# Copying shared rows two pairs ahead, and making the zeros for the first products first

## The chip, the core and the metric

The kernel runs on one core of a Trainium2 chip. The core has a matrix engine (TensorE, in the profile PE, with its weight loads as PEld), a vector engine (VectorE, DVE), a scalar engine (ScalarE, ACT), a general engine (GpSimd, POOL) and an engine that here only starts transfers (SyncE, SP). Each works through its own queue of instructions in order, and they wait for one another through semaphores. Data comes from the main memory (HBM) into SBUF by DMA; matrix products land in PSUM. The metric is the device time in microseconds (us) of one execution; the median of several executions is compared.

## What is computed

Attention over 64 pairs of batch and head, with a window of 32 keys (half of the heads) or every fourth of 128 keys (the other half), and then a mixture of experts with one expert per token. The expert is either the one that the token's own gate prefers or the one of the token before it.

```python
scores = scale * np.matmul(q, k.transpose(0, 1, 3, 2))
mask_plain = (rel >= 0) & (rel < window)
mask_dil = (rel >= 0) & (rel < window * dilation) & (rel % dilation == 0)
...
attn = np.exp(scores)
attn = attn / (np.sum(attn, axis=-1, keepdims=True) + 1e-09)
x = np.matmul(attn, v)
...
for b in range(B):
    prev_e = -1
    for s in range(S):
        fresh_e = int(np.argmax(logits[b, s]))
        if s == 0 or local_gate[b, s] < 0.5:
            e = fresh_e
        else:
            e = prev_e if prev_e >= 0 else fresh_e
        prev_e = e
        h = np.maximum(x[b, s] @ w1[e], 0.0)
        out[b, s] = p[e] * (h @ w2[e])
```

Batch 8, 8 heads of 64, 576 positions, so 4608 tokens of 512 features; 8 experts with 1024 hidden features; everything in 32-bit floats.

## The kernel before, in words

The heads are taken in pairs: there are 32 pairs of heads (`NPB`), each with its 576 positions in 9 blocks of 64. The heads with the wide window are reordered on the host, so that every head needs only a narrow band: a block of 64 queries looks at 96 keys, its own 64 and the 32 before them.

The function `whole` runs the kernel once with `exact` false; its result says whether a second, slower pass is needed, which a branch then runs (it isn't taken with this data). All of PE, DVE, POOL and SP are scheduled by hand: in each queue the instructions stand in the order in which the Python code makes them. The array `ones` is made ahead of that region, on DVE (L203). At the start of `whole`, DVE makes `zero` (L251), which POOL writes into one spare row of two buffers in the main memory (L253), and POOL clears a strip of the four `vt` tiles (L257). DVE then makes `warm`, an array of zeros of 128 by 512 (L281), and PE multiplies it by itself three times (`WARM`, L283) into a bank that nobody reads, before the first keys have come. After that DVE makes `before` (L300).

The attention loop (L1091) has one turn for each pair, and two more. In turn n, `scores(n)` multiplies keys and queries of pair n (L322 adds masks, L329), DVE and ACT make the exponentials `pr` (L334, L336); `share(n)` copies on POOL; then come `values(n - 1)`, the products of the exponentials with `vt` (L381), which DVE divides by their sums (L385, L386) into `x`. In every second turn `turn` transposes `x` on PE (L402, L406; ACT copies the result, L403), and `store` writes it to the main memory. `load(n + 3)` starts the transfers of keys and values three pairs ahead, from SP. The tile `vt` holds, for each block, 96 rows of values: the 64 rows of the block come by DMA, and the 32 rows ahead of it are the last ones of the block before. They are copied within SBUF by `share` (L270), one copy of 32 by 1040 elements for each pair. Four `vt` tiles are used in turn (`AHEAD`).

Between these steps `gap` takes steps of the routing from a list (`waiting`), by hand-written costs: gate logits (L433), the choice of experts (L445 to L516), the gates (L524 to L530), places within the expert (L540 and L541 on PE into the bank `kp`, L543 to L583 on DVE), and at two points the table of tokens for each expert. After the second of four groups of batches, the tokens of the first two units of expert work are known (`tokens`, L710 to L730), and the list `rows` is filled with eight gathers: POOL starts indirect DMAs that fetch rows of `x` by token number from the main memory into `xg` (L847). One gather is taken from the list at the end of each turn (L1116). So in the last turns of the attention loop POOL's queue has, in alternation, one copy (`share`) and one gather. PE uses the first four gathers in the last turn (L862), the others after the first expert's hidden products (L917).

The expert phase multiplies by the weights of the experts, 256 tokens at a time, with sums that save one product in eight (L943, L1025 with L810 to L819 on DVE).

The four PSUM banks of the attention phase are handed out in turn to `pv`, `tp`, `kp` and the other results of the routing; a product has to wait until the reader of the bank's earlier content is done.

Of the kernel before, what the change touches and what calls it, by code (L numbers as in the profile page):

```python
# [10 lines left out]
F32 = mybir.dt.float32  # L11
# [11 lines left out]
P = 128  # L23
# [14 lines left out]
NPB = B * NP  # L38
# [143 lines left out]
@with_exitstack  # L182
def dilated_attn_locality_moe_kernel(
    ctx: ExitStack,
    tc: tile.TileContext,
    qk: bass.AP,
    v: bass.AP,
    wgl: bass.AP,
    w1: bass.AP,
    w2: bass.AP,  # L190
    con: bass.AP,
    adm: bass.AP,
    msk: bass.AP,
    qmk: bass.AP,
    out: bass.AP,
):
    nc = tc.nc
    keep = ctx.enter_context(tc.tile_pool(name="keep", bufs=1))
    cst = keep.tile([P, C_ALL], F32, name="cst")
    wg = keep.tile([P, DK, LW], F32, name="wg")  # L200
    ones = keep.tile([P, P], F32, name="ones")
    bad = keep.tile([1, 1], I32, name="bad")
    nc.vector.memset(ones, 1.0)  # L203

    args = (qk, v, wgl, w1, w2, con, adm, msk, qmk, out, cst, wg, ones)
    again = whole(tc, False, bad, *args)

    with tc.If(again > 0):  # L208
        whole(tc, True, bad, *args)


@with_exitstack
def whole(ctx, tc, exact, bad, qk, v, wgl, w1, w2, con, adm, msk, qmk, out, cst, wg, ones):
    nc = tc.nc
    name = "exact" if exact else "plain"
    ctx.enter_context(tc.manual_schedule(engines={ET.PE, ET.DVE, ET.Pool, ET.SP}))
# [14 lines left out]
    def room(to, i, name, shape):  # L231
# [9 lines left out]
    ins, work, xp, xtp = (attention.enter_context(tc.tile_pool(name=name, bufs=bufs))  # L241
                     for name, bufs in (("ins", AHEAD), ("work", 2), ("xp", 3), ("xtp", 2)))
# [3 lines left out]
    def bank(shape, name):  # L246
        return banks.tile(shape, F32, name=name, tag="bank")
# [20 lines left out]
    def share(n):  # L268
        vt = vts[n % AHEAD]
        nc.gpsimd.tensor_copy(vt[:WIN, :, 1:], vt[QB:, :, :NB - 1])  # L270

    def load(n):
        load_keys(n)
        load_values(n)

    if not exact:
        am = work.tile([P, adm.shape[1]], BF16, name="am", bufs=1)
        nc.sync.dma_start(out=am, in_=adm)
        mk = work.tile([KW, 2, S - UNITS[1][0] * QB], BF16, name="mk", bufs=1)
        warm = work.tile([P, 512], F32, name="warm", bufs=1)  # L280
        nc.vector.memset(warm, 0.0)  # L281
        for _ in range(WARM):
            nc.tensor.matmul(bank([P, 512], "cold"), lhsT=warm[:, :P], rhs=warm, start=True, stop=True)  # L283
    load_keys(0)
# [17 lines left out]
    def load_first(i, part):  # L302

        rows = FK // 4
        nc.sync.dma_start(out=raw1[i][:, part * rows:(part + 1) * rows].rearrange("p m k f -> p (m k f)"),
                          in_=w1[i, :, part * rows * D:(part + 1) * rows * D])
# [60 lines left out]
    def values(n):  # L367

        vt = loaded[n][2]
        if n % 2 == 0:  # L370
            xs[n // 2] = xp.tile([P, SLOTS, 2, 2, DH], F32, name="x")
        x = xs[n // 2]
        pr = prob.pop(n)
        for a, z in HALVES:
            pv = bank([P, z - a, 2, VW], "pv")
            for k in range(a, z):
                for u in range(2):
                    for h in range(2):
                        i = min(2 * k + h, NB - 1)
                        c, p = next((c, p) for c, p in reversed(pr) if c <= i)  # L380
                        nc.tensor.matmul(pv[h * QB:(h + 1) * QB, k - a, u], lhsT=p[:, u, (i - c) * QB:(i - c + 1) * QB],  # L381
                                         rhs=vt[:, u, i], start=True, stop=True, tile_position=(0, h * QB),
                                         skip_group_check=True)
            r = rec[:, n, a:z]
            nc.vector.reciprocal(r, pv[:, :, :, DH])  # L385
            nc.vector.tensor_tensor(x[:, a:z, n % 2], pv[:, :, :, :DH],  # L386
                                    r.unsqueeze(3).to_broadcast([P, z - a, 2, DH]), op=Alu.mult)
        del loaded[n]

    def turn(m):  # L390

        x = xs[m]
        b, g = divmod(m, 2)
        if m % (2 * GB) == 0:
            routes[b // GB] = dict(xt=xtp.tile([P, 2, CH, GS], F32, name="xt"))
        xt = routes[b // GB]["xt"]
        s = b % GB * S
        full = S // P * P
        for c in range(CH):
            tp = bank([P, S // P, P], "tp")  # L400
            for k in range(S // P):
                nc.tensor.transpose(tp[:, k], x[:, k, c].rearrange("p u d -> p (u d)"), ident)  # L402
            nc.scalar.copy(xt[:, g, c, s:s + full], tp.rearrange("p k t -> p (k t)"))  # L403
        tp = bank([P, CH, S - full], "tp")
        for c in range(CH):
            nc.tensor.transpose(tp[:, c], x[:S - full, S // P, c].rearrange("p u d -> p (u d)"),  # L406
                                ident[:S - full, :S - full])
        nc.scalar.copy(xt[:, g, :, s + full:s + S], tp)

    def store(m):  # L410

        x = xs.pop(m)
        b, g = divmod(m, 2)
        full = S // P * P
        to = xd[g][b * S:(b + 1) * S]
        nc.sync.dma_start(out=to[:full].rearrange("(k p) f -> p k f", p=P),
                          in_=x[:, :S // P].rearrange("p k g u d -> p k (g u d)"))
        nc.sync.dma_start(out=to[full:], in_=x[:S - full, S // P].rearrange("p g u d -> p (g u d)"))
# [360 lines left out]
    def gap(add=None):  # L779
        if add is not None:  # L780
            credit[0] = min(credit[0] + add, add)
        alone = False
        while waiting and not alone and (add is None or credit[0] >= 0):
            f, cost, _ = waiting.pop(0)
            credit[0] -= cost
            if f:
                f()
            alone = add is None or not waiting or waiting[0][2]
# [7 lines left out]
    def now(push):  # L796
        for f in push:
            f()
# [55 lines left out]
    def features(u):  # L854
        kind = units[u]["kind"]
        rows = rows_in(u)
        xe[u] = mw.tile([P, DK, 2 * P], F32, name="xe")
        for j in range(tiles_of(u)):
            x = xg.pop((u, j)).rearrange("p g f -> p (g f)")
            tp = bank([P, DK, P], "tp")  # L860
            for kk in range(DK):
                nc.tensor.transpose(tp[:, kk, :rows], x[:rows, kk * P:(kk + 1) * P], ident[:rows, :rows])  # L862
            nc.scalar.copy(xe[u][:, :, j * P:j * P + rows], tp[:, :, :rows])
        if kind == "pair":
            xc[u] = mw.tile([P, 4, DK // 2, P], F32, name="xc", bufs=1)
            return sums_right(xc[u], *(xe[u][:, 2 * k:2 * k + 2, j * P:(j + 1) * P]
                                       for k in range(2) for j in range(2)))
        return []
# [222 lines left out]
    for n in range(NPB + 2):  # L1091
        if n < NPB:
            (scores_exact if exact else scores)(n)
        if n < NPB:
            share(n)
        gap(SHARE)
        if 1 <= n <= NPB:
            values(n - 1)
        if n == NPB + 1:
            assert len(rows) <= 4  # L1100
            now(features(0))
        if n >= 3 and n % 2 == 1:
            turn((n - 3) // 2)
            if (n - 3) // 2 % (2 * GB) == 2 * GB - 1:
                route((n - 3) // 2 // (2 * GB), n == NPB + 1)
        gap(SHARE)
        if n + 3 < NPB:
            load(n + 3)
        if n >= 3 and n % 2 == 1:
            store((n - 3) // 2)  # L1110
        if n in (11, 14, 17, 20):
            load_first(0, (n - 11) // 3)
        if n == NPB + 1:
            weights(0, True)
            weights(1, False)
        if rows:  # L1116
            rows.pop(0)()
# [161 lines left out]
```

## Time and profile before

| | |
|---|---|
| median of 3 executions | 675.02 us (674.6 to 676.7) |
| the profiled execution | 672.8 us |
| its span, first to last instruction | 670.9 us |
| mean granted PE clock in it | 0.995 of full |
| bytes by DMA, mean rate | 126.38 MB, 188 GB/s |

The attention phase takes the span's first 158 us or so, the experts the rest. A line of the timeline gives the start (us from the span's start), the length, the engine, the line of the kernel, the operation, its output and inputs, how many of them were merged, and in brackets how long the engine had been idle before and what ended that. In a list of waits, each line names who waited for whom, then us in total, how many times, and the longest. In a table of windows each line is a stretch of time with the busy time of each engine in it, the granted clock of PE (1.00 is full), the share of time in which the DMA engines were busy, and what they moved.

The start of the kernel on DVE, in the timeline (the three arrays, then `before`):

```profile
0.85 0.17 DVE L203 MEMSET ones<- 128x128 f32 x1 [0.85 <-PEq L1271]
1.01 0.27 DVE L251 MEMSET zero<- 1x256 f32 x1
1.33 0.48 DVE L281 MEMSET warm<- 128x512 f32 x1
1.77 0.07 DVE L300 MEMSET before<- 96x8 f32 x1
```

And on PE, the first products and the first scores:

```profile
1.87 4.78 PE L283 MATMUL cold<-warm 128*128 128x512 f32 x6 [1.87 <-DVE before L300]
6.58 0.34 PE L322 MATMUL two<-am 64*96 64x320 bf16 x2
6.76 1.67 PE L329 MATMUL two<-kq 64*96 64x64 f32 x36
```

### The profile page before, as it was taken

To read this page: it belongs to the slowest core of one execution; us is meant where nothing else is said; L and a number is where in the kernel's file an instruction comes from. 1 tells how busy PE (TensorE), PEld (TensorE's weight loads), DVE (VectorE), ACT (ScalarE), POOL (GpSimd) and SP (SyncE) were. 2 spreads that over 40 slices of the span, in tenths; PEclk is the share of its full clock that TensorE was granted. 3 is DMA by queue.
4 is the path that set the end of the run, shared out by engine and by line. 5 is a ranking of instruction groups with operands and counts; after the bars stand their busy time and mean duration, and the time that the engine had idled before them with its cause. 6 is when DMAs were issued, how large, how long until landed. Compare 5 with 4: busy or idle time off the path is not lost. (4 is left out here: it accounts for less than half of the span.)

```text
span 670.9 us, 15284 instructions
## 1 busy us (share of the span) xinstructions
PE 655.1 (98%) x6466; PEld 572.1 (85%) x6466; DVE 373.7 (56%) x755; ACT 188.7 (28%) x348; POOL 186.6 (28%) x162
## 2 busy tenths in 40 slices
PE   8999999999999999999999999999999999999996
PEld 6988888787769999999589989997889988899893
DVE  3548669474397587363455581727373637446441
ACT  3544343432112232322223213222222232213210
POOL 3322212132023420321560343414044213041011
PEclk9999999999999999999999999999999999999999
DMA  8989889746403289666452545741054452353001
GB/s 325 321 274 310 279 263 324 244 138 240 196 33 146 91 355 386 228 221 214 140 233 75 219 173 185 288 143 60 9 189 166 182 218 98 123 221 145 1 33 49
DMA packets 29357, 126.38 MB, mean 188 GB/s; under 512 B 4221, under 2 KB 13789, under 8 KB 25312
## 3 DMA queue, kind: packets, MB, share of 16 engines
q1 hardware_dynamic: 22480, 106.10, 43.7%
q0 software_dynamic: 6800, 19.21, 8.3%
q8 instruction: 53, 0.87, 0.5%
q14 instruction: 24, 0.20, 0.1%
HBM read 142.07 MB, written 19.20 MB: 240 GB/s over the span
## 5 line engine op out<-in xcount | busy, mean ns | idle before, releaser
L971 POOL DMA_INDIRECT out_dram<-y,tok x36 | 55.0, 1528 | 297.0 <-DVE y L1040 124.0
L943 PE MATMUL hp<-xc,sum 128*128 128x128 f32 x720 | 85.6, 276 | 0.4 <-DVE sum L810 0.4
L943 PEld LDWEIGHTS hp<-xc,sum 128*128 128x128 f32 x720 | 82.8, 192 | 0.8 <-PE hp L943 0.5
L1025 PE MATMUL yp<-sum,hc 128*128 128x256 f32 x360 | 82.7, 380 | 0.0
L953 DVE TENSOR_TENSOR h<-hp,h 128x512 f32<-128x512 f32 x45 | 30.9, 690 | 90.4 <-PE hp L943 89.7
L1025 PEld LDWEIGHTS yp<-sum,hc 128*128 128x128 f32 x360 | 68.3, 190 | 9.6 <-ACT y L1033 0.4
L1040 DVE SCALAR_TENSOR_TENSOR y<-yp,gate,y 128x256 f32<-128x256 f32 x45 | 21.7, 482 | 75.3 <-issue 48.1
L270 POOL COPY vt<-vt 32x1040 f32<-32x1040 f32 x32 | 34.5, 1081 | 95.8 <-DMA vt<-in_v_dram 67.8
L943 PE MATMUL hp<-xe,raw 128*128 128x128 f32 x480 | 58.8, 276 | 0.0
L943 PEld LDWEIGHTS hp<-xe,raw 128*128 128x128 f32 x480 | 56.6, 192 | 1.8 <-issue 1.5
L1025 PE MATMUL yp<-raw,h 128*128 128x256 f32 x240 | 57.0, 381 | 0.0
L847 POOL DMA_INDIRECT xg<-xd,tok x40 | 46.0, 1149 | 38.1 <-PE hp L943 15.3
L329 PE MATMUL two<-kq 64*96 64x64 f32 x1152 | 54.9, 245 | 0.0
L329 PEld LDWEIGHTS two<-kq 64*96 64x96 f32 x1152 | 52.8, 162 | 0.0
L1025 PEld LDWEIGHTS yp<-raw,h 128*128 128x128 f32 x240 | 44.5, 190 | 5.5
L947 ACT COPY h<-hp 128x512 f32<-128x512 f32 x45 | 26.3, 585 | 79.3 <-PE hp L943 75.4
L334 DVE SCALAR_TENSOR_TENSOR pr<-two,mk 96x512 f32<-96x512 f32 x32 | 21.9, 684 | 47.9 <-ACT pr L336 37.7
L381 PE MATMUL pv<-vt,pr 96*64 96x65 f32 x1280 | 46.1, 226 | 2.1 <-POOL vt L270 1.6
L847 POOL DMA_INDIRECT xg<-xd,pos x40 | 44.2, 1104 | 12.1 <-issue 10.7
L954 ACT ACTIVATE h<-h 128x512 f32<-128x512 f32 x45 | 28.3, 630 | 67.2 <-DVE h L953 67.2
L381 PEld LDWEIGHTS pv<-vt,pr 96*64 96x64 f32 x1280 | 41.0, 139 | 5.1 <-POOL vt L270 1.9
L1033 ACT ACTIVATE y<-yp,gate 128x256 f32<-128x256 f32 x45 | 21.2, 473 | 56.1 <-PE yp L1025 50.0
(222 smaller groups left out, 1013.4 us busy)
## 6 DMA issues: line engine op xcount, KB each, us to landing
raw<-in_w_dram SPq DMA_DIRECT2D x48, 2048.0 KB
kq<-in_qk_dram SPq DMA_DIRECT2D x32, 592.0 KB
vt<-in_v_dram SPq DMA_DIRECT2D x32, 292.5 KB
xd<-x SPq DMA_DIRECT2D x16, 512.0 KB
raw<-in_w_dram SPq DMA_DIRECT2D x4, 512.0 KB
xd<-x SPq DMA_DIRECT2D x16, 64.0 KB
xg<-xd,tok POOLq DMA_INDIRECT x40, 3.2
xg<-xd,pos POOLq DMA_INDIRECT x40, 3.3
```

The costliest lines, as they stand in the source:

```text
L270: nc.gpsimd.tensor_copy(vt[:WIN, :, 1:], vt[QB:, :, :NB - 1])
L329: nc.tensor.matmul(sc[:KW, u, (i - a) * QB:(i - a + 1) * QB], lhsT=kt[h, i * QB:i * QB + KW], rhs=qt[h, i * QB:(i + 1) * QB], start=bool(a ...
L334: nc.vector.scalar_tensor_tensor(pr, sc[:KW, :, :w], -CEIL, mk[:, kind].unsqueeze(1).to_broadcast([KW, 2, w]), Alu.max, Alu.min)
L381: nc.tensor.matmul(pv[h * QB:(h + 1) * QB, k - a, u], lhsT=p[:, u, (i - c) * QB:(i - c + 1) * QB], rhs=vt[:, u, i], start=True, stop=True, ...
L847: nc.gpsimd.indirect_dma_start(out=x[:rows, g], out_offset=None, in_=xd[g] if units[u]["late"] else xd[g][:EARLY * GS], in_offset=bass.Ind ...
L943: nc.tensor.matmul(to[:, m], lhsT=a[:, m, kk], rhs=b[:, kk], start=first and m == 0 and kk == 0, stop=(kk == DK // 2 - 1), skip_group_chec ...
L947: nc.scalar.copy(at((0, 1, 3)[k]), of)
L953: nc.vector.tensor_tensor(at(k), of, at(k), op=Alu.add)
L954: nc.scalar.activation(at(k), at(k), Act.Relu)
L971: nc.gpsimd.indirect_dma_start(out=out, out_offset=bass.IndirectOffsetOnAxis(ap=of_unit(u, "tok", j), axis=0), in_=y, in_offset=None, boun ...
L1025: nc.tensor.matmul(to, lhsT=a[:, m], rhs=b[:, m], start=first and m == 0, stop=(m == FK // 2 - 1), skip_group_check=True)
L1040: nc.vector.scalar_tensor_tensor(at(k), of, of_unit(u, "gate", k // 2), at(k), Alu.mult, Alu.add)
```

## The change

The array `warm` is no longer made inside `whole`, in the pool that lives during attention, but ahead of everything, in the pool that is kept throughout; its memset is the first of DVE's. And the copies of shared rows are made two pairs ahead of the values that need them instead of one: turn 0 makes copies 0 and 1, and turn n makes copy n + 1.

```diff
     bad = keep.tile([1, 1], I32, name="bad")
+    warm = keep.tile([P, 512], F32, name="warm")
+    nc.vector.memset(warm, 0.0)
     nc.vector.memset(ones, 1.0)
 
-    args = (qk, v, wgl, w1, w2, con, adm, msk, qmk, out, cst, wg, ones)
+    args = (qk, v, wgl, w1, w2, con, adm, msk, qmk, out, cst, wg, ones, warm)
...
         mk = work.tile([KW, 2, S - UNITS[1][0] * QB], BF16, name="mk", bufs=1)
-        warm = work.tile([P, 512], F32, name="warm", bufs=1)
-        nc.vector.memset(warm, 0.0)
         for _ in range(WARM):
             nc.tensor.matmul(bank([P, 512], "cold"), lhsT=warm[:, :P], rhs=warm, start=True, stop=True)
...
     for n in range(NPB + 2):
         if n < NPB:
             (scores_exact if exact else scores)(n)
-        if n < NPB:
-            share(n)
+        for k in range(NPB)[n + 1 if n else 0:n + 2]:
+            share(k)
         gap(SHARE)
         if 1 <= n <= NPB:
             values(n - 1)
```

More of the change, by code (lines that the diff above doesn't have):

```diff
@@ L212, in whole @@
 @with_exitstack
-def whole(ctx, tc, exact, bad, qk, v, wgl, w1, w2, con, adm, msk, qmk, out, cst, wg, ones):
+def whole(ctx, tc, exact, bad, qk, v, wgl, w1, w2, con, adm, msk, qmk, out, cst, wg, ones, warm):
     nc = tc.nc
```

## The prediction

> **What bounds the kernel now.** I read the busy table first, then what TensorE (PE) waits for, then the timeline of GpSimd (POOL) and of PE around the longest such wait, and last the granted clock there.
>
> ```profile
> PE 655.1 (98%) x6466; PEld 572.1 (85%) x6466; DVE 373.7 (56%) x755; ACT 188.7 (28%) x348; POOL 186.6 (28%) x162
> ```
> ```profile
> PE cold L283 <- DVE before L300: 1.9, 1, 1.9
> PE hp L943 <- DVE h L953: 1.7, 2, 0.9
> PE pv L381 <- POOL vt L270: 1.6, 2, 1.2
> ```
> PE sets the end: it is busy for 98% of the span and its longest waits (us in total, times, longest) come to a few us. No PE wait on a transfer of `kq`, `vt` or weights is in that list, so a microsecond that PE gets back early should reach the end. The change bears on the first and third line. The third sits where POOL's row gathers (L847) and the copies of shared rows (L270) alternate:
>
> ```profile
> 126.89 1.04 POOL L847 DMA_INDIRECT xg<-xd,tok  x1 [12.77 <-DVE gate L730]
> 131.81 1.04 POOL L270 COPY vt<-vt 32x1040 f32<-32x1040 f32 x1 [3.88 <-issue]
> 133.12 1.01 POOL L847 DMA_INDIRECT xg<-xd,pos  x1 [0.27 <-DMA xd<-x]
> 136.99 1.04 POOL L270 COPY vt<-vt 32x1040 f32<-32x1040 f32 x1 [2.86 <-PE two L329]
> 138.30 0.97 POOL L847 DMA_INDIRECT xg<-xd,tok  x1 [0.27 <-POOL vt L270]
> 142.47 1.04 POOL L270 COPY vt<-vt 32x1040 f32<-32x1040 f32 x1 [3.20 <-PE two L329]
> 143.78 0.97 POOL L847 DMA_INDIRECT xg<-xd,pos  x1 [0.27 <-POOL vt L270]
> 147.38 1.04 POOL L270 COPY vt<-vt 32x1040 f32<-32x1040 f32 x1 [2.62 <-PE two L329]
> 148.69 1.04 POOL L847 DMA_INDIRECT xg<-xd,tok  x1 [0.27 <-POOL vt L270]
> 151.62 1.04 POOL L270 COPY vt<-vt 32x1040 f32<-32x1040 f32 x1 [1.89 <-PE tp L402]
> ```
> These are copies 27 to 31. Each starts 2.9 to 4.9 us after the gather ahead of it. The built program says why: in this stretch every copy also waits for the semaphore of that gather's landing, and landing takes 2.7 to 4.8 us (median 3.5); the PE named as releaser is only what came last in the trace. What that does to PE, and to its clock (columns of the last two lines: stretch and its length, busy us of PE, PEld, DVE, ACT, POOL, clock, DMA share, GB/s):
>
> ```profile
> 143.57 1.38 PE L381 MATMUL pv<-vt,pr 96*64 96x65 f32 x38 [0.39 <-POOL vt L270]
> ...
> 148.47 1.86 PE L381 MATMUL pv<-vt,pr 96*64 96x65 f32 x38 [1.23 <-POOL vt L270]
> 150.26 1.97 PE L402 MATMUL tp<-cst,x 128*128 128x128 f32 x8
> ```
> ```profile
> 145.76:149.17 3.41, 2.19 (x55) 1.98 (x53) 2.85 (x12) 1.33 (x2) 1.52 (x2) 1.00 0.58 195
> 149.17:152.59 3.42, 3.42 (x33) 2.85 (x29) 1.44 (x5) 0.91 (x2) 1.53 (x2) 0.50 0.14 38
> ```
> Right after a window in which PE worked 2.19 of 3.41 us, its clock is half for 3.42 us. So the stall is paid twice: as idle time, and as slow matmuls after it.
>
> [...] L567 takes 943 to 946 ns but 1436 beside the copy at 106.21, and L525 takes 168 ns but 460 at 147.99, ending just after the copy of 147.38 does. [...]
>
> **Copies two pairs ahead.** The same 32 copies in the same order, 1.04 us each. Copies 0 to 26 keep their place in POOL's queue and their waits (no other POOL instruction stands between them), so nothing moves there. Only the stretch above changes: copy 27 goes ahead of the first gather, and copies 28 to 31 take the places of 27 to 30. Of the queues, POOL's alone is reordered; SP's loads keep their order and waits, and no wait is added on PE. The first gather now stands behind copy 27. Its rows were asked for at 113.78; those of copy 26 (asked for at 109.17) were there by 113.08, so it should run near 118, long before the tokens are known (126.89). The gathers then keep their times, and so do the copies' slots: 131.81 for copy 28, 136.99 for 29, 142.47 for 30, 147.38 for 31. The products that need them (values 28 to 31) began at 137.76, 142.85, 146.92, 153.07, each after the end of its new slot. The slot at 151.62 is empty, so the last three gathers come some 3 us earlier; their rows are first used at 178.75.
>
> What PE gets back, from starts of its groups against the same groups undisturbed (values 1.32 us from 126.53 to 127.85; eight transposes 1.02 to 128.87; two more 0.26):
> - values 28: 137.76 to 139.40 is 1.64, so 0.32 of stall;
> - values 29: 142.85 to 144.88 is 2.03, so 0.71;
> - values 30: 146.92 to 150.26 is 3.34, so 2.02, of which 0.54 is slow clock (38 products took 1.79, not 1.25): 1.48 stall;
> - transposes 1.90 and 0.40, the two `kp` products 0.51 instead of 0.34: 0.88 + 0.14 + 0.17 of slow clock.
>
> Stall 2.51, clock 1.73 (half of 3.42 is 1.71), together 4.24 us if only PE counted. DVE is late next. Its work in the iteration of values 30 starts from PE's `cp` product, which moves 1.03 earlier, but L506 must follow the L386 of values 29, so DVE reaches L516's end near 146.2, L334's (0.69) near 146.85; then L524 to L530 (1.64, less 0.29 if L525 is not held) and the first L385 and L386 (0.62) end near 148.8. PE's `kp` (L540) reuses the bank that this L386 empties: it goes near 148.9 instead of 152.56, 3.7 earlier. If copy 31, at 147.38, holds L527 [...] to its end at 148.42, `kp` goes near 149.9: 2.7 earlier. I take the middle, 3.2, and keep 2.7 and 3.7. The later DVE steps (L543 to L567, 2.7 us, ahead of the next L385) follow `kp` and carry the same shift on. The loads issued from 158.29 follow DVE's last `x` and move along.
>
> **Zeros first.** No operation is added. The memset of `warm` (0.48 us) starts at 0.85 in place of 1.33, so the first product goes near 0.85 + 0.48 + 0.06 (today's gap after its end) = 1.39, not 1.87. `ones`, `zero`, `before` follow 0.5 later; behind `zero` wait two 1 KB writes and the memsets of `vt` (end 3.5, then 4.0), and the first copy starts at 8.78 by its transfer. The six cold products are 0.85 apart, the last 0.59 us long: slow, then fast. If the clock rises at the same instant, 0.48 us earlier at half speed is worth 0.24; if it rises a window sooner, up to 1.7 more; if the first keys are not there, nothing. They should be: `am` and `kq` are 680 KB, and the DMA view's slices of 0.75 us add up to that by about 4.5 us, while PE takes them at 6.58. I take 0.3, bounds 0 and 1.7. The later home of `warm`, 2 KB per partition held throughout, moves other tiles; the waits of PE, DVE, ACT and SP are unchanged but for this one, so I price it at 0.
>
> **Sum.** 3.2 + 0.3 = 3.5 us: the profiled execution goes from 672.8 (span 670.9) to 669.3 (667.4). The median of the runs shown is 2.2 above it; the same difference gives 675.0 - 3.5 = 671.5.
>
> **Rivals.**
> 1. DVE takes over and the clock still falls. If L527 is held, PE waits some 1.1 us for L386. A window with 3.02 of 3.41 us busy (141.41 to 144.82) cost no clock, one with 2.19 did; this would have about 2.3. Then 1.7 is lost again and the gain is 2.7 + 0.3 - 1.7 = 1.3: 673.7. For it: DVE stands full there; against: L527 has to come a moment after the copy.
> 2. The timed executions had no clock drop. [...] Without the 1.73 the gain is 1.0 to 2.0 + 0.3, say 1.7: 673.3. For it: this is one execution; against: a stall of 1.48 fits whole into most positions of a 3.41 window, and the timed ones are slower, not faster.
> 3. Slower: the lock between copies and DVE. Four moved copies lie beside other DVE work; each can hold DVE for 1.04, 4.16 in all, and PE follows DVE's `x`. If all of it came on the path, with the clock drop kept and one added (1.7), the time is 675.0 - 2.5 - 0.3 + 4.2 + 1.7 = 678.1. It decides once held time and clock exceed the 2.8 us of stall saved by 2. Against: the moved copies only fill slots that copies filled before, and L525 was held 0.29.
>
> **How the numbers follow.** Forecast 0.62, rival 1 0.17, rival 2 0.15, rival 3 0.06. About 0.3% (2.0 us, so 673.0 and 677.0) is what a measurement of this kernel can tell. Faster: nearly all of the forecast (0.60), a third of rival 2, a little of rival 1: 0.68. Slower 0.06, the rest 0.26. The range runs from 669.9 (the PE sum of 4.24 with a better start) to 673.9, past rivals 1 and 2.
>
> **What would show it.** Copies 28 to 31 near 131.8, 137.0, 142.5, 147.4; no PE wait on `vt`; transposes of the iteration after values 30 in about 1.0 us at clock 1.00; first product near 1.4; L540 at 148.6 to 149.6. Wrong if PE waits for L386 by over 1 us there, if the clock falls elsewhere, or if the first scores don't start before 6.58.

## The result, and the profile after

| | median us | executions |
|---|---|---|
| before | 676.67 (674.6 to 680.52) | 14 |
| changed | 677.35 (673.34 to 678.67) | 14 |

The ratio is 0.9996, 95% interval 0.9977 to 1.0015: no difference that can be told. The ratios, here and below, leave out executions more than 1.5% above the fastest of their kernel, and need not equal the quotient of the medians. The profiled execution took 677.08 us (span 675.2, clock 0.994), against 672.8 of the profiled one before, which was quicker than every timed execution of its own kernel.

The busy table of the changed kernel, first line, and four lines of its list of waits:

```profile
PE 656.2 (97%) x6466; PEld 573.0 (85%) x6466; DVE 373.5 (55%) x755; ACT 189.1 (28%) x348; POOL 186.3 (28%) x162
```
```profile
PE tp L406 <- ACT xt L403: 3.4, 4, 2.7
PE hp L943 <- DVE h L953: 1.7, 2, 0.9
PE cold L283 <- DVE warm L204: 1.5, 1, 1.5
...
PE tp L402 <- issue: 0.8, 3, 0.3
```

The wait on `vt`, 1.6 us before, is gone, and the first product starts at 1.47 instead of 1.87. New at the top is one wait of 2.7 us for ACT's copy L403. POOL's timeline shows the moved copies (the four lines of `vt` are copies 28 to 31) and what became of the last gathers:

```profile
131.83 1.05 POOL L272 COPY vt<-vt 32x1040 f32<-32x1040 f32 x1 [3.42 <-DMA xg<-xd,tok]
...
137.28 1.04 POOL L272 COPY vt<-vt 32x1040 f32<-32x1040 f32 x1 [3.13 <-PE pv L381]
...
141.48 1.04 POOL L272 COPY vt<-vt 32x1040 f32<-32x1040 f32 x1 [1.91 <-PE tp L402]
...
145.73 1.04 POOL L272 COPY vt<-vt 32x1040 f32<-32x1040 f32 x1 [1.97 <-PE cp L502]
147.04 1.10 POOL L847 DMA_INDIRECT xg<-xd,tok  x1 [0.27 <-POOL vt L272]
148.45 0.95 POOL L847 DMA_INDIRECT xg<-xd,pos  x1 [0.30 <-issue]
149.70 0.94 POOL L847 DMA_INDIRECT xg<-xd,tok  x1 [0.30 <-issue]
150.95 0.95 POOL L847 DMA_INDIRECT xg<-xd,pos  x1 [0.30 <-issue]
```

Copies 28 to 31 stand where copies 27 to 30 stood, the last two 1.0 and 1.7 us earlier. The last four gathers run back to back. While they run, the timelines of PE, ACT and DVE show this:

```profile
150.62 0.38 PE L402 MATMUL tp<-cst,x 128*128 128x128 f32 x2 [0.17 <-issue]
153.65 0.47 PE L406 MATMUL tp<-cst,x 64*128 64x64 f32 x2 [2.65 <-ACT xt L403]
...
153.01 1.07 ACT L403 COPY xt<-tp 128x512 f32<-128x512 f32 x2 [3.93 <-remote]
...
152.95 0.20 DVE L385 RECIPROCAL rec<-pv 128x6 f32<-128x6 f32 x1 [1.67 <-remote]
```

PE's eight transposes are done at 151.0, but ACT starts to copy them at 153.01, and DVE takes up products of before 149 at 152.95: the trace's semaphore events have PE's increment for those products at 152.92, with two more within 0.12 us after it. (In after_again, below, the same increments come 0.01 to 0.03 us after the recorded end of their product.) So PE's signals reach both engines 2 us or more late, and the profile names only "remote" as what ended the waits. The windows of that stretch (columns as in the prediction):

```profile
148.39:151.80 3.41, 1.81 (x20) 1.17 (x14) 1.76 (x9) 0.63 (x1) 2.74 (x3) 1.00 0.58 170
151.80:155.21 3.41, 1.56 (x11) 1.28 (x13) 0.93 (x3) 1.34 (x3) 0.10 (x1) 0.50 0.20 58
155.21:158.63 3.42, 3.42 (x46) 3.30 (x45) 3.11 (x13) 0.18 (x1) 0.00 (x0) 0.50 0.00 0
```

The window with this stall is followed by two at half clock. So a stall was taken away and another one stood in its place. The question for the experiments is whether the change makes the second stall (**theory G**: the gathers that lose the copy between them), or whether such stalls come and go in either kernel (**theory C**).

### The profile page after: what moved, and what is told of

Read it like the earlier page. It is cut to its first block, busy times and chain, and to the rows that moved or that the text cites. A ratio compares the mean times of both kernels' runs of the same rounds, so it can differ in the third digit from the quotient of the medians.

```text
span 675.2 us, 15285 instructions
## 1 busy us (share of the span) xinstructions
PE 656.2 (97%) x6466; PEld 573.0 (85%) x6466; DVE 373.5 (55%) x755; ACT 189.1 (28%) x348; POOL 186.3 (28%) x162
```

## The experiments

Each kernel was timed beside the kernel before, on one chip per group. "Low clock" counts executions with a mean granted clock under 0.9965. Profiled executions that run at half clock only at their start and end have 0.997 to 0.999; one more window of 3.41 us at half clock costs 1.7 us of 670, or 0.0025, as an estimate from the half clock. So the count can miss an execution whose only fall lasted one window. In groups 1, 3, 4 and 5 the executions of before with a low clock took 3.4 to 5.4 us more, in the median, than the others.

| group, chip | kernel | median us | before, same group | ratio, 95% interval | low clock | low clock of before |
|---|---|---|---|---|---|---|
| 1, chip 9 | before_again | 671.98 | 671.25 | 0.9992 (0.9966 to 1.0017) | 6 of 22 | 18 of 75 |
| | after_again | 670.33 | | 0.9985 (0.9963 to 1.0007) | 6 of 22 | |
| | copies_alone | 671.12 | | 0.9988 (0.9962 to 1.0013) | 6 of 22 | |
| | zeros_alone | 671.37 | | 0.9993 (0.9970 to 1.0016) | 8 of 22 | |
| 2, chip 2 | ahead_on_act | 681.87 | 678.16 | 1.0059 (1.0036 to 1.0082) | 7 of 7 | 25 of 42 |
| | behind_on_act | 681.15 | | 1.0033 (1.0008 to 1.0058) | 12 of 12 | |
| | copied_twice | 680.99 | | 1.0072 (1.0038 to 1.0106) | 14 of 14 | |
| | zeros_late | 678.56 | | 1.0016 (0.9995 to 1.0037) | 16 of 22 | |
| 3, chip 4 | after_third | 670.89 | 672.23 | 0.9975 (0.9946 to 1.0003) | 2 of 14 | 11 of 44 |
| | after_spaced | 670.00 | | 0.9971 (0.9956 to 0.9986) | 2 of 23 | |
| | on_act_spaced | 669.37 | | 0.9952 (0.9935 to 0.9970) | 0 of 11 | |
| | burst_of_8 | 669.78 | | 0.9950 (0.9924 to 0.9976) | 2 of 10 | |
| 4, chip 3 | act_second | 668.84 | 671.53 | 0.9960 (0.9944 to 0.9977) | 1 of 22 | 18 of 67 |
| | burst_second | 669.25 | | 0.9961 (0.9946 to 0.9976) | 4 of 24 | |
| | act_spaced_second | 669.57 | | 0.9971 (0.9955 to 0.9987) | 1 of 22 | |
| | after_fourth | 670.15 | | 0.9992 (0.9968 to 1.0015) | 4 of 14 | |
| 5, chip 7 | one_on_act | 670.12 | 672.77 | 0.9960 (0.9938 to 0.9982) | 0 of 22 | 15 of 34 |
| | four_on_act | 669.55 | | 0.9938 (0.9915 to 0.9961) | 0 of 13 | |

### The parts, and the same kernels again

`before_again` and `after_again` are the two kernels unchanged. `copies_alone` has only the second part of the diff, `zeros_alone` only the first:

```diff
# copies_alone
-        if n < NPB:
-            share(n)
+        for k in range(NPB)[n + 1 if n else 0:n + 2]:
+            share(k)
# zeros_alone: warm made in the kept pool, its memset ahead of that of ones
```

> The kernel before, unchanged, for a second profile and more times. Theory G (the gathers): the wait of 2.65 us for L403 in turn 31 of the changed kernel comes from the gathers that no longer have a copy between them, so it is absent here: copies 29 and 30 again hold PE for 0.4 and 1.2 us, at most one clock window at half speed in the middle, 674 to 677. Theory C (chance): stalls of 2 to 4 us in the last turns of attention come and go from execution to execution in either kernel, and the first profile was one without: then this profile may show one too, and times spread over 674 to 681 as before.

> The changed kernel, unchanged, for a second profile. Theory G: the wait for L403 in turn 31 (about 2.7 us) and two clock windows at half speed come back in the same place; 676 to 678. Theory C: this profile may be free of them; then the attention ends 2.5 to 3.5 us earlier than in the first profile of the kernel before, and the time is near 671 to 673.5.

> Only the copies go two pairs ahead; the zeros are made where they were. Both theories: first product at 1.9 us. Theory G: as the whole change, less 0.3 us: wait for L403 of over 2 us in turn 31, ratio 0.998 to 1.003. Theory C: no fixed place for the stall; the ratio is below 1 by what the copies' stall was worth on the mean, 0.995 to 0.999.

> Only the zeros are made first; copies one pair ahead as before. Both theories: first product near 1.4 us, first scores 0.25 to 0.6 us earlier, copies 29 and 30 hold PE as before. Ratio 0.998 to 1.001 (0.3 us of 675 is 0.05%).

The wait for L403 did not come back with the same gathers. PE's timeline of after_again at that place:

```profile
147.44 1.39 PE L381 MATMUL pv<-vt,pr 96*64 96x65 f32 x40
148.76 1.09 PE L402 MATMUL tp<-cst,x 128*128 128x128 f32 x8
150.09 0.33 PE L406 MATMUL tp<-cst,x 64*128 64x64 f32 x2 [0.24 <-ACT xt L403]
150.35 0.41 PE L540 MATMUL kp<-oh,cst 96*96 96x96 f32 x2
150.86 1.39 PE L381 MATMUL pv<-vt,pr 96*64 96x65 f32 x40
```

Theory G as it stood falls: four gathers in a row don't by themselves stop anything on chip 9. What each execution needs from the first product of values 27 to the logits after the last transposes (first L433 after values 31) sorts the profiles:

| us from values 27 to L433 | half clock in it | |
|---|---|---|
| before, before_again | 3.41, 10.24 us | 23.33, 25.61 |
| zeros_alone (copies not ahead) | none | 21.69 |
| after_again, copies_alone | none | 20.56, 20.34 |
| after | 6.83 us | 25.42 |

Where the clock holds, the copies ahead are worth 1.1 to 1.4 us of that stretch (1.3 to 1.7 with the later after_fourth and after_third, 20.43 and 20.01), with zeros_alone as the only profile of the old order that has neither a fall nor late signals there; against the execution that the forecast was made from, 2.8 to 3.0. These profiles fit theory C on the falls: in before_again the fall at this place lasted three windows where it had lasted one, and zeros_alone, with the copies where they were, has none here, and one of 10.24 us at 72.56 instead.

### Twice the stall, and a later start

```diff
# copied_twice
         if n < NPB:
             share(n)
+        if n in (28, 29, 30):
+            share(n)
# zeros_late
-        nc.vector.memset(warm, 0.0)
+        for _ in range(3):
+            nc.vector.memset(warm, 0.0)
```

> The kernel before with the copies of turns 28, 29 and 30 done twice, so that each of these three stalls grows by up to 1.04 us (0.32, 0.71, 1.48 in the first profile; 1.36, 1.75 and 2.52 here). Prediction's view (a stall of about 1.5 us costs its own length and a half-speed window of 3.41 us, 1.7 us more): 3.1 us of stall and two windows more than before, median 3 to 7 us above, and nearly every execution at a clock under 0.9965. Rival [...]: some 3 us above, and the share of executions under 0.9965 stays near the 27 of 100 of the runs so far.

> The kernel before with the memset of warm done three times, so the first product starts near 2.9 us in place of 1.87. Theory D (the first three turns are held by the arrival of kq of turn 2 near 15.4 to 15.8 us, whenever PE begins): values 2 still starts within 17.2 to 18.1 us and the median is within 0.5 us of before. Prediction's view (each us later at half speed is worth half a us): values 2 0.5 us later, median 0.5 us above; if the clock rises a window later, 2.2 above.

`copied_twice` costs 2.8 us in the medians, and all of its 14 executions have a low clock (25 of 42 of before, beside it). One line of its waits, and its windows:

```profile
PE pv L381 <- POOL vt L270: 3.8, 3, 2.1
```
```profile
149.26:152.67 3.41, 1.57 (x40) 1.50 (x41) 2.92 (x9) 0.63 (x1) 2.69 (x3) 1.00 0.40 130
152.67:156.08 3.41, 3.41 (x26) 2.79 (x26) 1.29 (x4) 1.34 (x3) 1.65 (x2) 0.50 0.14 38
```

The waits more than double, and a window with 1.57 of 3.41 us busy is followed by half clock. So in this profile a longer stall at this place is paid twice, as the prediction said; that all 14 executions fell at this place and for this reason is not shown, only that all have a low clock. The difference of the medians lies just under the expected 3 to 7, and the interval of the ratio is 2.6 to 7.2 us. On `zeros_late` I expected values 2 at 17.2 to 18.1 us; it started at 18.58, but act_second and act_spaced_second, with the zeros as before, started it at 18.58 and 18.59. So it isn't shown that the later start (3.19 for 1.87) comes through to turn 2, and the median shows 0.4 us, within its interval of nothing.

### The copies on ACT

```diff
# ahead_on_act from the changed kernel, behind_on_act from the kernel before
-        nc.gpsimd.tensor_copy(vt[:WIN, :, 1:], vt[QB:, :, :NB - 1])
+        nc.scalar.copy(vt[:WIN, :, 1:], vt[QB:, :, :NB - 1])
```

The reason for this pair lay at turns 14 to 16. DVE and POOL in zeros_alone, with PE after them, from their timelines:

```profile
65.82 1.80 DVE L567 TENSOR_TENSOR lane<-cst,lanes 96x768 f32<-96x768 f32 x1
...
65.77 1.04 POOL L272 COPY vt<-vt 32x1040 f32<-32x1040 f32 x1 [1.10 <-DMA vt<-in_v_dram]
...
72.05 0.31 PE L406 MATMUL tp<-cst,x 64*128 64x64 f32 x2 [1.99 <-DVE rec L385]
```

And in after_again:

```profile
65.94 0.94 DVE L567 TENSOR_TENSOR lane<-cst,lanes 96x768 f32<-96x768 f32 x1
...
65.97 1.83 POOL L272 COPY vt<-vt 32x1040 f32<-32x1040 f32 x1 [1.19 <-PE pv L381]
```

Where the copy starts 0.05 us ahead, L567 takes 1.80 us; where L567 starts 0.03 ahead, it takes 0.94 and the copy 1.83. DVE has no idle time from 65 to 74 us, so what it loses reaches PE at L406, and at 72.56 the clock falls. This copy is number 16, the same in both kernels.

> The changed kernel with the 32 copies of shared rows on ACT in place of POOL (ACT takes 1.05 us for two copies of 512 columns, so some 1.1 us for one of 1040). Theory L (a POOL copy and DVE hold each other, and whichever loses decides the stalls of 2 us at turns 15 and 16): DVE's L567 takes 0.94 to 0.95 us at all four places (1.20 to 1.80 at some of them in the runs so far), no copy takes over 1.2, values 14 to values 16 takes 10.7 to 11.1 us, and the median is 1 to 2 us under that of the changed kernel, with fewer executions under clock 0.9965 than the 27 of 100 of all runs so far. Theory C (the stalls come from something that neither kernel sets[...]): median within 1 us of the changed kernel's and the same share of executions with a lower clock.

> The kernel before with only the engine of the copies changed from POOL to ACT; share(n) stays in turn n. Theory Q (what the changed loop gains is only that copies no longer queue behind the gathers): the waits of PE on vt go here too, with copies not moved ahead, values 27 to the end of attention takes 20.3 to 20.6 us as with copies ahead (21.7 to 25.6 behind the gathers), and the median equals that of the same edit with copies ahead within 0.7 us. Rival A (the copies must also be earlier by a turn): PE waits on vt remain, values 27 to the end takes 21 us or more.

Both were slower than before, and not for the reason in either expectation. Four lines of the waits of behind_on_act after 126 us, and its ACT timeline:

```profile
ACT xt L403 <- remote: 9.5, 1, 9.5
...
PE lp L433 <- remote: 7.0, 1, 7.0
DVE rec L385 <- remote: 6.6, 1, 6.6
POOL xg L847 <- issue: 2.1, 7, 0.3
```
```profile
127.62 0.63 ACT L336 ACTIVATE pr<-pr 96x512 f32<-96x512 f32 x1
137.80 1.07 ACT L403 COPY xt<-tp 128x512 f32<-128x512 f32 x2 [9.55 <-remote]
```

With no copies in POOL's queue, all eight gathers ran back to back (126.09 to 135.92), and PE, DVE and ACT stood still for some 7 us (called the hold below); PE had done the transposes that ACT waits for at 129.6, and DVE goes on at 136.15, just after a semaphore event of PE at 136.13. This gave **theory B**: gathers back to back delay PE's signals, on some chips or executions; in the kernel before, copies stood between them. ahead_on_act has the same hold, 7.08 us of PE. L567 took 0.94 or 0.95 at all four places in both, as theory L said, and values 14 to 16 took 10.46 (behind) and 10.76 us (ahead). The wait on `vt` was gone without copies ahead, as theory Q said: with the copies off POOL's queue, they need not come a turn earlier.

### Gathers one by one, or all together

`after_third` is the changed kernel. `after_spaced` and `on_act_spaced` (from behind_on_act) add a tiny copy that waits for each of the first eight gathers; `burst_of_8` sends these eight together:

```diff
# after_spaced, on_act_spaced, at the end of part()
+            if u < 2:
+                nc.gpsimd.tensor_copy(space, x[:1, g, :1])
# burst_of_8
-        if rows:
+        if rows and n >= NPB:
             rows.pop(0)()
+        if n == NPB:
+            while len(rows) > 4:
+                rows.pop(0)()
```

> The changed kernel once more, as a control beside the next three, on the same chip. Theory B (gathers back to back on POOL can delay PE's semaphores to DVE and ACT, on some chips or executions; in the kernel before, copies stood between them and spaced them out, and the change takes the copy from between the last four): where the trace shows PE semaphores over 2 us late elsewhere (as in the first session, where the median was 677), turn 31 has a wait of L406 or L403 of 2 to 3 us while the last four gathers run; where it shows none (median near 670 to 671), there is no such wait. Rival C (those waits come by chance): a wait at turn 31 has nothing to do with late semaphores elsewhere.

> The changed kernel plus a copy of one element of each gathered block on POOL, which waits for that gather to land, after each of the first eight gathers; so no two of them run back to back. Theory B: the last four gathers start 3 to 5 us apart instead of 1.25, no wait of PE, DVE or ACT over 0.5 us at turn 31, values 27 to the end of attention 20.3 to 20.7 us; the median 1 to 5 us under after_third where semaphores are late, and equal to it within 0.5 us where they are not. Rival C: the same median as after_third in either case.

> Copies on ACT, as in behind_on_act (share(n) in turn n), with the same spacing of the first eight gathers. Theory B: the hold of 7 us after 129 us, in which PE, DVE and ACT all stood still while eight gathers ran back to back, is gone; values 14 to 15 stays at 4.6 us (5.2 and more with copies on POOL), so the median is 7 to 12 us under behind_on_act beside the same kernel before, and 1 to 2 us under that kernel. Rival C: the hold of 7 us remains, since ACT's place in the order causes it and not the gathers.

> The changed kernel with its first eight gathers issued together after the last copy, copies still on POOL. Theory B: the eight run back to back from about 146 to 157 us; where semaphores are late PE, DVE and ACT stand still for 5 to 9 us and the clock falls, so the median is 5 to 9 us over after_third; the hold needs no copies on ACT. Rival C (the order of ACT's queue caused the hold of behind_on_act): no hold here, median within 1 us of after_third.

On this chip no profile had a late signal or a hold. Eight gathers ran back to back in burst_of_8 (143.01 to 152.86), and no wait of PE in that profile is over 1.6 us; on_act_spaced had no hold either, but with the spacing the chip had changed too. So this group couldn't decide on the hold between B and its rival, called C in these expectations (the order of ACT's queue). `burst_of_8` was no loss but 1.1 us under after_third in the medians (0.9 under after_fourth in the next group), within what 10 and 14 executions can tell. Its copies 28 to 31 no longer wait for gathers to land, but from values 28 to 29 both profiles took 4.77 us, so the gain isn't traced to that. after_spaced was 0.9 us under after_third, more than the 0.5 expected; its profiled execution (span 681.2) had two falls, at 73.03 and 117.40, the first after an L567 of 1.82 us.

> behind_on_act once more, on the same chip as the next three. Theory B (the hold of 7 us comes from gathers back to back where PE's semaphores can be late, so it goes with the chip): held here if and only if burst_second is held too; where the trace has no late semaphores there is no hold, values 26 to 27 takes 8.0 us (17.1 in behind_on_act) and the median is 668 to 670 for a before of 671 to 672. Rival C (ACT's order causes it): held here whatever the chip, 10 us over act_spaced_second.

> burst_of_8 once more. Theory B: no hold where the trace has no late semaphores, and one of 5 to 9 us where it has. Rival C: no hold on any chip.

> on_act_spaced once more. Theory L with B: the shortest of all on either kind of chip, 2 to 3 us under before, with hardly an execution under clock 0.9965, since neither a copy and DVE hold each other nor gathers run back to back. Rival: the 11 executions without a fall were luck; then a fifth to a quarter of them are under 0.9965, as with copies on POOL.

> The changed kernel as the control of this call: 0.5 to 1.3 us under before where semaphores are not late, equal to before or above it where they are (turn 31 with a wait of 2 us or more).

These are behind_on_act, burst_of_8, on_act_spaced and the changed kernel once more. In act_second the same program as behind_on_act ran its eight gathers back to back (126.35 to 136.18) with no hold, as the PE timeline shows:

```profile
127.89 1.09 PE L402 MATMUL tp<-cst,x 128*128 128x128 f32 x8
128.91 0.33 PE L406 MATMUL tp<-cst,x 64*128 64x64 f32 x2
129.18 3.19 PE L433 MATMUL lp<-xt,wg 128*32 128x288 f32 x32
```

Its L433 starts at 129.18, that of behind_on_act at 137.09. The order of ACT's queue is the same, so this rival falls: the hold goes with the chip or its condition. Copies on ACT, once 3 us slower than before, are here 2.7 us faster. act_spaced_second was to be the shortest of all; it was not (669.57, act_second 668.84).

### The one copy

```diff
# one_on_act, from the changed kernel; four_on_act: n in (16, 17, 24, 25)
-        nc.gpsimd.tensor_copy(vt[:WIN, :, 1:], vt[QB:, :, :NB - 1])
+        copy = nc.scalar.copy if n == 16 else nc.gpsimd.tensor_copy
+        copy(vt[:WIN, :, 1:], vt[QB:, :, :NB - 1])
```

> The changed kernel with copy 16 alone on ACT, the one that stands beside DVE's first L567 near 66 us (it held L567 to 1.41 to 1.82 us in 8 of the 13 profiles with it on POOL, and was itself held to 1.29 to 1.83 in 4). Theory L (that coin toss starts most falls of the clock): L567 0.94 to 0.95 at 66 us, values 14 to values 16 10.5 to 11.1 us in the profile, and clearly fewer executions under clock 0.9965 than the fourth to a quarter of before in the same call. Rival: the falls come from elsewhere, and the share stays near a quarter.

> The changed kernel with copies 16, 17, 24 and 25 on ACT (those beside L567, L577 and L583 in both routes), the other 28 on POOL, where copies 28 to 30 still stand between gathers. Theory L: nearly no execution under clock 0.9965, median 668.5 to 670 beside a before of 671 to 672, as with all copies on ACT, and no hold of 7 us after 129 us on any chip. Rival: what helped with all copies on ACT was something else (the free POOL queue), and the median stays within 0.5 us of the changed kernel's, 1 us under before.

One copy out of 32 moved: no low clock in 22 executions, against 15 of 34 of before in the same group and 18 of 72 of the same loop with all copies on POOL in other groups (after_again, copies_alone, after_third, after_fourth). The changed kernel itself was not timed on chip 7, so its share there is not known. With all copies on ACT it was 2 of 55 (on_act_spaced, act_second, act_spaced_second). one_on_act's DVE timeline has the product undisturbed (the line number has moved by one); values 14 to 16 took 11.15 us, though, just over the expected 10.5 to 11.1:

```profile
66.71 0.94 DVE L568 TENSOR_TENSOR lane<-cst,lanes 96x768 f32<-96x768 f32 x1
```

`four_on_act` beats the kernel before: 669.55 beside 672.77, ratio 0.9938 (0.9915 to 0.9961), while the changed kernel stayed within the interval of no change in each of its groups. That it beats the changed kernel too is likely but not shown, as the two were never timed together. Against copies on ACT throughout, it still has copies 28 to 30 between the gathers; whether that helps where signals are late was not run.

## Why the prediction was wrong

It forecast 671.5 us and 3.5 us of gain. The medians of the changed kernel (and copies_alone) lie 0.9, 0.1, 1.3 and 1.4 us under before on chips 9, 4 and 3, where each ratio's interval includes no change, and 0.7 above it in the first session.

- **Copies two pairs ahead: the mechanism was right.** No profile of the changed kernel or copies_alone has a wait of PE on `vt`. DVE was late next, as said: from values 27, `kp` (L540) comes after 15.07 and 15.10 us (after_again, copies_alone), against 18.07 before, so 3.0 earlier where 3.2 (2.7 to 3.7) was taken; against zeros_alone, where the clock holds there (16.32), it is 1.2. Its absolute time, 150.35, is later than the 148.6 to 149.6 that was to show it, since values 27 itself started 0.8 later.
- **What went wrong is the term "clock 1.73" of the sum, and the step that carries it to the median: "The median of the runs shown is 2.2 above it; the same difference gives 675.0 - 3.5 = 671.5".** The stall's half-speed window was taken as part of every execution, and as gone for good once the copies' stall is gone ("transposes ... in about 1.0 us at clock 1.00"). Neither held. In the first session's profile of the changed kernel another stall, of 2.65 us, stood at the same place, and the clock fell there for 6.83 us where it had been 3.42. In groups 1, 3, 4 and 5, only 28% of the timed executions of before have a low clock at all (68 of 242, the 22 of before_again among them), and with copies ahead it is 25% (18 of 72; 20%, 26 of 129, with after_spaced and the two bursts): the change hardly cured falls. That most start at copy 16 is what one_on_act suggests, and its place is the same in both kernels; in the profiles 4 of 11 falls (without the two holds) came there, 3 at 110 to 117 us and 4 in the last turns. Without the clock the stretch gives back 1.1 to 1.7, of which the medians show 0.1 to 1.4.
- **Rival 2** ("The timed executions had no clock drop"), held at 0.15, is what happened in seven of ten executions on those four chips; its gain of 1.7 was still too much. For the first session it can't be checked: the clocks of before's executions there are not on record. Its counter-argument, that the timed executions were slower, looked at the time and not at the clock of executions.
- **Rival 3** named the lock of copies and DVE as the way to lose, and found it not to matter. It does, in two ways. Copy 29 in its new slot (137.44) meets DVE's L466 in after_again, from the timelines:

```profile
137.45 1.05 DVE L466 TENSOR_TENSOR code<-code,own 96x12 f32<-96x12 f32 x1
...
137.44 1.04 POOL L272 COPY vt<-vt 32x1040 f32<-32x1040 f32 x1 [2.57 <-PE pv L381]
```

  L466 took 0.17 us in behind_on_act. So from values 28 to values 29 it takes 5.35 us in after_again. The four profiles with copies ahead in which copy 29 held L466 (after, after_again, after_fourth) or L461 (copies_alone) took 5.34 to 5.35; in after_third L466 started first, the copy took 1.15, and it was 4.77, as in four_on_act, where no such meeting took place. So 0.6 us of the stall got back is lost where DVE comes second. The larger way is copy 16, which the forecast did not look at, since the change leaves it alone.
- **Rival 1** (a wait for L386) is not what cost it: PE waits there for 0.2 to 0.4 us at a time in after_again. Its window with 3.02 us busy (141.41 to 144.82) lies across two windows of the clock; the clock's own, 142.35 to 145.76, has 3.02 too, so the comparison stands.
- **Zeros first.** 0.3 us is neither shown nor excluded. The first product starts at 1.47 (forecast 1.39: the memset starts at 0.93, not 0.85), the first scores at 5.63 in zeros_alone, not 6.58. But values 2 starts between 17.2 and 18.6 us in either sort of kernel: on average 17.63 in 11 profiles with zeros first and 17.92 in 8 with the old order (without zeros_late). When the clock first rises varies more (4.3 to 8.1 us), and no early start brought values 2 ahead of 17.2; in zeros_alone PE waits 0.64 us for the keys of pair 2.
- **The first session** has something that no rival had: signals of PE 2 us late. There the changed kernel lost 2.65 us and two windows of half clock at the place where it had gained. 12 of its 14 executions have a low clock. Its chip is not on record; chip 2 showed such signals too, and its before (678.16) was about as slow.

**What stays open.** Why PE's signals are late. The traces say what they go with. Matching PE's 499 increments with the semaphore events in order, 42 come more than 0.5 us after the recorded end of their product: 8 or 9 in each of after, ahead_on_act, behind_on_act, copied_twice and zeros_late (all but the first on chip 2), and none in the other fifteen profiles. All 42 belong to products that end while POOL issues an indirect DMA (a gather, or later a scatter), or within 1.0 us after it; this takes a third of the span and holds 26% of PE's increments. A single gather can have a small delay beside it: one at 139.26 in zeros_late, a signal 0.65 us late at 139.9. In the two holds of 7 us DVE goes on 0.2 to 0.3 us after the eighth gather ends. In after, DVE's and ACT's own signals, as far as they match an event, come at most 0.03 and 0.01 us after the recorded end. So on chip 2 and in the first session the late signals go with POOL's indirect DMAs, in a row or alone; that is theory B, and more. Two reservations remain: the same five profiles lack 22 to 40 semaphore events of PE, DVE and ACT (the others at most 4), so the matching is an estimate; and chips 9, 4, 3 and 7 run the same gathers without any of this. What sets chip 2 apart is not known, and neither a burst of gathers with copies on POOL nor spaced gathers were run there, so what spacing would save is not shown.

## What to carry to other kernels

Before a stall's price is taken from a profile, look at the granted clock of each timed execution: it tells how many of them had the fall that the profiled one had. In 12 of 13 profiles copy 16 on POOL and DVE's L567 started 0.03 to 0.56 us apart, and one of them was held: L567 in 8, the copy in 4. Where such a pair shows in a profile and DVE is full, try that one copy on another engine: one_on_act left no low clock in 22 executions. And an instruction between two transfers in a queue can be a spacer: the sixth gather started 4.25 us after the fifth in the kernel before, with copy 31 between them, and 1.41 after it in the changed one. Say what runs back to back once the spacer is gone.

## What the runs showed of the hardware

- **Of copy 16 and L567, the one that started second was held, even 0.03 us behind.** Of 13 profiles with copy 16 on POOL, L567 was the held one in 8 (1.41 to 1.82 us instead of 0.94) and the copy in 4 (1.29 to 1.83 instead of 1.04), each time the one that started second, by 0.03 to 0.56 us. In the thirteenth, copied_twice, L567 started 0.89 us after the copy and took 0.97. Of the 8, values 14 to 16 took 11.5 to 11.9 us in 4, and 15.2 to 18.0 with two to five half-speed windows in the other 4; where the copy was held, 11.1 to 11.2. What sets apart the DVE instructions that a copy holds is not shown: beside the copy of 147.38 in before, L525 took 0.46 us instead of 0.17, and L524, at 147.72, 0.24, as it did in after with no copy beside it.
- **The windows that a fall followed were 33 to 73% busy, and the busy share alone doesn't tell whether the clock will fall.** The windows lie on a grid of 3.413 us from the clock's first rise, in every profile: in before the clock was full for 143.36 us, half for 3.41 and full for 515.41, which is 42, 1 and 151 windows. Before the end of the kernel, the windows that a fall followed had 1.12 to 2.49 us of 3.41 busy (2.19 in before, 1.81 in after, 1.57 in copied_twice). None with more was followed by one, but of those with less some were not: 2.47 in after_again, 1.98 in copied_twice, and 1.78 in after_third:

```profile
69.11:72.52 3.41, 1.78 (x34) 1.47 (x30) 3.38 (x7) 1.36 (x3) 0.52 (x1) 1.00 0.95 267
72.52:75.93 3.41, 3.35 (x81) 3.24 (x82) 3.31 (x7) 1.72 (x4) 0.60 (x2) 1.00 1.00 376
```

- **In after_fourth the clock stayed at half through five windows in which PE was busy throughout.** Falls lasted one to five windows (3.41 to 17.07 us), so a fall can cost more than the one window that the prediction counted. The first two of after_fourth, with 3.42 and 3.41 us busy:

```profile
72.61:76.03 3.42, 3.42 (x54) 3.30 (x53) 2.19 (x5) 1.33 (x2) 0.65 (x1) 0.50 1.05 402
76.03:79.44 3.41, 3.41 (x30) 3.29 (x27) 1.04 (x3) 0.00 (x0) 0.40 (x1) 0.50 0.64 215
```

- **The same program had PE, DVE and ACT held on one chip and not on another.** In behind_on_act on chip 2 one wait each of PE, DVE and ACT took 7.0, 6.6 and 9.5 us beside eight gathers, and L433 started at 137.09; in act_second on chip 3 it started at 129.18, and no wait of PE is over 1.9 us.
